# GpSimd's operations wait for the VectorE operation that the plan put before them at the shared port

## The chip, the cores and the metric

One core of a Trainium2 chip runs one program. The metric is the device time of one execution in microseconds (us): median of three runs 697.6, from 697.25 to 699.5. One further execution was profiled; it took 697.67.

The engines: TensorE (PE, its weight loads PEld) multiplies into PSUM, VectorE (DVE) and ScalarE (ACT) read PSUM and SBUF, GpSimd (POOL) works on SBUF alone, SyncE (SP) issues DMAs. Each engine runs its own queue in order and waits on semaphores that others raise.

## The reference

Attention with a threshold, then a gated mix, all in float32 (8 batches, 8 heads, 576 positions, 64 wide):

```python
scores = scale * np.matmul(q, k.transpose(0, 1, 3, 2))
thresh = np.max(scores, axis=-1, keepdims=True) - tau
scores = np.where(scores >= thresh, scores, -1000000000.0)
attn = np.exp(scores - np.max(scores, axis=-1, keepdims=True))
attn = attn / (np.sum(attn, axis=-1, keepdims=True) + 1e-09)
x = np.matmul(attn, v)   # heads side by side: (8, 576, 512)
gate_pre = sum(conv_w[k] * xp[:, k:k + S] for k in range(5))   # xp: x behind 4 rows of zeros
out = (1 / (1 + np.exp(-gate_pre))) * (x @ w_val) @ w_out
```

## The kernel before

The heads go in 32 pairs (8 batches of 4). Per pair nine score tiles, most of 128 x 576, are made by TensorE (L594), scaled into SBUF with their largest value by VectorE (L601, tile sb), and turned into weights: a threshold th (L611 on VectorE or GpSimd, L609 on ScalarE), an exponential e on ScalarE (L617, L619), and the cut, either on VectorE (L636: keeps e where sb is under th, tile pp or pl, with the row's sum) or on ScalarE (L630). L657 takes reciprocals of the sums, L667 on GpSimd or L665 on ScalarE widens them to inv, TensorE turns the weights (L724), ScalarE copies them out (L736), TensorE multiplies by v (L797), and VectorE writes the pair's xT (L806).

Then the pair's mix: xh and xl, the high and low part of xT (L840 or L342, and L846 on GpSimd), and the convolution: tap 0 on GpSimd (L859, tile pre), the others on VectorE (L864), in a few early pairs one of them as L879 and L885 on GpSimd. Per batch two products of 512 x 512 (L955), between them g (L993), its parts gh (L1016, ScalarE) and gl (L1024, GpSimd).

In the first 150 us the two weight matrices are also rebuilt from 64-bit words by `from_f64`: on VectorE L355, L357, L359, L361 and L368, on GpSimd L366, L371 and L417.

What sets the order: every piece is an `op` with an engine, a cost and a due number. `carry_out` plays all of them through once, at build time: it takes the operation that can begin first by the costs, moves the engine's clock on, and at the end emits all in that order. VectorE has two names there. "DVE" is an operation with an operand in PSUM (or a tiny one); "DVEp" is one on SBUF alone, with two large inputs or int32 words. DVEp and POOL share one clock, `port`: in the plan no two of them ever run at the same time. The emitted program knows nothing of `port`: an operation waits for its data and its rooms (the buffers, `Rooms`), and for nothing else.

Of the kernel before, what the change touches and what calls it, by code (L numbers as in the profile page):

```python
# [33 lines left out]
for x in range(6):  # L34
# [10 lines left out]
    s=3,  # L45
# [33 lines left out]
def tile_thresholded_attention_gated_mix(  # L79
# [14 lines left out]
    nc = tc.nc  # L94
# [86 lines left out]
    port = [0.0]  # L181
# [15 lines left out]
    def keep_busy(room, n, x=ident):  # L197

        for _ in range(n):
            nc.tensor.matmul(room[:, 0:P], x, x, start=True, stop=True)  # L200

    def sent(t, n, latency, each):

        at = t
        for _ in range(n):
            if len(landings) >= 8:
                at = max(at, landings[-8])
            wire[0] = max(wire[0], at + latency) + each
            landings.append(wire[0])
            at += SEND  # L210
        return at - t, wire[0] - t

    def carry_out():
        done_ops = []
        while True:
            best = None
            for e, ops in open_ops.items():
                can = []
                free = idle[e.rstrip("p")]
                if e in ("DVEp", "POOL"):  # L220
                    free = max(free, port[0])
                for o in ops:
                    if all(r.times for r in o.takes):
                        can.append((max([free, o.ready] + [r.times[0] for r in o.takes]), o))
                if can:
                    t = min(x for x, _ in can)
                    o = min((x[1] for x in can if x[0] <= t), key=lambda o: o.due)
                    if best is None or (t, o.due) < (best[0], best[1].due):
                        best = (t, o, e)
            if best is None:  # L230
                break
            t, o, e = best
            for x in o.ways:
                open_ops[x].remove(o)
            if e == "PE" and 0.0 < idle["PE"] and t < FILL_UNTIL and r_s.times:
                pause = t - max(idle["PE"], r_s.times[0])
                if pause > 0.8:
                    o.fill = int((pause - 0.6) / 0.24)
            cost, done, emit = o.ways[e]
            if e == "PE" and cost:  # L240
                extra = CHANGE.get((shape[0], o.shape), 0.0)
                cost, done = cost + extra, done + extra
                shape[0] = o.shape
            if isinstance(done, tuple):
                cost, done = sent(t, *done)
            if e in ("DVEp", "POOL"):
                port[0] = t + cost
            e = e.rstrip("p")
            idle[e] = t + cost
            o.landed, o.engine = t + done, e  # L250
            done_ops.append((o, emit))
            for r in o.takes:
                r.times.pop(0)
            for r, _ in o.gives:
                r.times.append(o.landed)
                r.times.sort()
            for n in o.next:
                n.ready = max(n.ready, idle["PE"] if e == "PE" and e in n.ways else o.landed)
                n.waits -= 1
                if not n.waits:  # L260
                    for x in n.ways:
                        open_ops[x].append(n)
        assert not any(open_ops.values()), "some operations can never begin"
        for o, emit in done_ops:
            if o.fill:
                keep_busy(r_s.free[0][1][:, 0, :], o.fill)
            emit()
            for rooms, room in o.gives:
                rooms.give(room(), o.landed)

# [244 lines left out]
    class Tile:  # L515
        s = None
# [45 lines left out]
        def room(self):  # L562

            if self.s is None:
                self.s = self.grp.second
            return self.s
# [536 lines left out]
    at = 0  # L1103
# [6 lines left out]
    for t in jobs:  # L1110
# [21 lines left out]
        if t.pair.g == NP - 1:  # L1132
            last = products(batch, len(tiles), last)
    carry_out()


# [57 lines left out]
```

## Time and profile before

| | |
|---|---|
| median of the runs | 697.6 us |
| profiled execution | 697.67 us |
| its span | 695.9 us |
| PE busy | 664.3 us |
| DVE busy | 596.1 us |
| ACT busy | 587.4 us |
| POOL busy | 249.5 us |

The span is what the profile covers; 1.8 us of the execution lie around it. "Busy" is time in which the engine has an instruction running, also one that is held up, which shows as one that took long. The chain of work that ended last goes back from the last instruction, at each step to what released it. A row of the timeline gives start, duration, engine, line, operation and tiles; a bracket at its end is idle time of that engine before it and what ended it. From about 170 us on the rows repeat with each batch, every 81.0 us.

### The profile page before, as it was taken

How to read it: one execution, taken by the hardware profiler on the slowest of the kernel's cores; microseconds unless marked ns; L12 is line 12 of the kernel's file. 1: busy time of each engine (PE TensorE's matmuls, PEld its weight loads, DVE VectorE, ACT ScalarE, POOL GpSimd, SP SyncE). 2: the span in 40 equal slices, each digit the busy share in tenths (PEclk: the TensorE clock that was granted, in tenths of full speed). 3: DMA queues.
4: the chain of work that ended last, by engine and by line, in shares of the span. 5: the costliest groups of instructions: out<-in, count | busy, mean ns of one | idle time of the engine just before them, and what ended most of it. 6: DMA issues, size and time to landing. Idle time of an engine off the chain costs nothing.

```text
span 695.9 us, 21477 instructions
## 1 busy us (share of the span) xinstructions
PE 664.3 (95%) x8610; PEld 521.8 (75%) x8610; DVE 596.1 (86%) x1598; ACT 587.4 (84%) x1206; POOL 249.5 (36%) x404
## 2 busy tenths in 40 slices
PE   8877889999999999999999999999999999999997
PEld 5544557667887777888787788877778887777897
DVE  6988989998888898988979989888989889799642
ACT  6998989999889988998879989799889988799620
POOL 2554555673222620433222422226214332224231
PEclk9999999999999999999999999999999999999999
DMA  7123333023321233223222233311332232220102
GB/s 266 51 96 108 123 116 103 33 70 117 118 87 29 78 120 102 84 86 103 64 94 86 68 120 103 103 40 66 120 106 82 85 104 75 83 86 1 53 19 70
DMA packets 21076, 61.19 MB, mean 88 GB/s; under 512 B 2928, under 2 KB 4336, under 8 KB 20976
## 3 DMA queue, kind: packets, MB, share of 16 engines
q1 hardware_dynamic: 20832, 59.62, 25.3%
q8 instruction: 68, 1.11, 0.7%
q14 instruction: 32, 0.26, 0.1%
q10 hardware_dynamic: 144, 0.20, 0.1%
HBM read 50.37 MB, written 9.44 MB: 86 GB/s over the span
## 4 chain that ended last, share of the span: by engine, by line
PE 53%; DVE 27%; ACT 13%; issue 6%; DMA 0%; DVEq 0%; ACTq 0%
PE u L955 19%; PE u L797 14%; DVE sb L601 12%; PE u L594 11%; DVE pp L636 8%; PE u L724 7%; ACT e L619 3%; ACT T L736 3%; ACT pp L630 3%; PE u L768 2%; ACT e L617 2%; DVE pre L864 2%; DVE r L657 1%; DVE pl L636 1%; ACT inv L665 1%
## 5 line engine op out<-in xcount | busy, mean ns | idle before, releaser
L601 DVE TENSOR_SCALAR_CACHE_REDUCE sb<-u,sc 128x576 f32<-128x576 f32 x288 | 228.0, 809 | 26.2 <-PE u L594 13.9
L594 PE MATMUL u<-k,q 64*128 64x288 f32 x1240 | 190.0, 418 | 5.1 <-DVE sb L601 3.3
L736 ACT COPY T<-u 128x512 f32<-128x512 f32 (+1 forms) x256 | 169.9, 688 | 13.2 <-PE u L724 12.4
L636 DVE SCALAR_TENSOR_TENSOR pp<-sb,th,e 128x577 f32<-128x577 f32 x164 | 145.0, 892 | 16.1 <-ACT e L619 15.3
L619 ACT ACTIVATE e<-sb,nm 128x576 f32<-128x576 f32 x193 | 146.6, 772 | 3.5 <-DVE sb L601 1.3
L797 PE MATMUL u<-T,v 128*64 128x256 f32 (+1 forms) x1080 | 136.9, 408 | 2.0 <-ACT T L736 2.0
L724 PEld LDWEIGHTS u<-ident,pp 64*128 64x128 f32 x2304 | 102.8, 139 | 46.1 <-ACT T L736 9.8
L594 PEld LDWEIGHTS u<-k,q 64*128 64x128 f32 x1240 | 108.4, 187 | 29.5 <-DVE sb L601 8.9
L724 PE MATMUL u<-ident,pp 64*128 64x64 f32 x2304 | 114.7, 226 | 15.3 <-DVE sb L601 7.8
L797 PEld LDWEIGHTS u<-T,v 128*64 128x64 f32 x1080 | 75.1, 137 | 54.4 <-ACT T L736 3.1
L864 DVE SCALAR_TENSOR_TENSOR pre<-xT,cw,pre 128x576 f32<-128x576 f32 x121 | 107.7, 890 | 1.7 <-POOL pre L859 0.9
L955 PE MATMUL u<-xh,wvh 64*128 64x288 f32 x512 | 87.3, 326 | 0.9 <-ACT seen L943 0.3
L955 PE MATMUL u<-gh,woh 64*128 64x288 f32 x512 | 84.1, 316 | 0.9 <-ACT T L744 0.6
L617 ACT ACTIVATE e<-sb,th 128x576 f32<-128x576 f32 x95 | 73.3, 775 | 8.0 <-DVE th L611 5.3
L955 PE MATMUL u<-xh,wvl 64*128 64x288 f32 x512 | 78.7, 291 | 0.0
L955 PE MATMUL u<-xl,wvh 64*128 64x288 f32 x512 | 78.6, 291 | 0.0
L955 PE MATMUL u<-gh,wol 64*128 64x288 f32 x512 | 77.9, 291 | 0.0
L955 PE MATMUL u<-gl,woh 64*128 64x288 f32 x512 | 77.9, 291 | 0.0
L630 ACT ACTIVATE pp<-e,minus 128x576 f32<-128x576 f32 x92 | 71.2, 774 | 0.7 <-DVE pp L636 0.2
L1024 POOL TENSOR_TENSOR gl<-g,gh 128x288 fp32r<-128x288 f32 x64 | 58.9, 935 | 31.8 <-ACT gh L1016 31.6
L667 POOL TENSOR_SCALAR inv<-r 128x128 f32<-128x128 f32 x79 | 25.0, 316 | 123.8 <-DVE r L657 106.1
L955 PEld LDWEIGHTS u<-xh,wvh 64*128 64x128 f32 x512 | 51.1, 185 | 6.4 <-DVE xT L806 3.3
(92 smaller groups left out, 992.7 us busy)
## 6 DMA issues: line engine op xcount, KB each, us to landing
q<-qT SPq DMA_DIRECT2D x31, 608.0 KB, 4.1
k<-kT SPq DMA_DIRECT2D x31, 496.0 KB, 5.0
v<-vs SPq DMA_DIRECT2D x32, 320.0 KB, 2.9
outT<-o SPq DMA_DIRECT2D x28, 288.0 KB, 2.2
pre<-w_val SPq DMA_DIRECT2D x4, 512.0 KB, 6.9
pre<-w_out SPq DMA_DIRECT2D x4, 512.0 KB, 3.5
outT<-o SPq DMA_DIRECT2D x8, 144.0 KB, 1.8
pp<-first SPq DMA_DIRECT2D x2, 192.0 KB, 3.0
```

The source lines that it names most:

```text
L594: nc.tensor.matmul(row(self.s)[:, a, :], t.q[rows, x : x + P], t.k[rows, k0 : k0 + HS], start=i == 0, stop=h is not None or i == 1, skip_g ...
L601: nc.vector.tensor_scalar(self.sb[:, :S].rearrange("p (a f) -> p a f", a=2), row(self.room()), sc, None, op0=ALU.mult, op1=ALU.min, accum_ ...
L617: nc.scalar.activation(y, x, AF.Prelu, bias=self.th, scale=-1.0, alpha=STEEP)
L619: nc.scalar.activation(y, x, AF.Exp, bias=self.nm, scale=-1.0)
L630: nc.scalar.activation(grp.p[:, i * S : (i + 1) * S], self.e[:, :S], AF.Exp, bias=minus, accum_out=grp.sums[:, i : i + 1])
L636: nc.vector.scalar_tensor_tensor(grp.p[:, i * S : (i + 1) * S + 1], self.sb, self.th, self.e, op0=ALU.is_le, op1=ALU.mult, accum_out=grp.s ...
L724: nc.tensor.transpose(tp[:, r, i * APART_BY : i * APART_BY + D], x[rows, :], ident[rows, rows])
L736: engine(T[:, c0 : c0 + n, self.off : self.off + P].rearrange("p c (r q) -> p r c q", r=2), tp)
L797: nc.tensor.matmul(a[hs, : W[half.j]], t.v[:, c0 : c0 + D], half.T[:, 2 * NKC if c == NKC else h * NKC + c, 0 : W[half.j]], start=c == 0, ...
L864: engine.scalar_tensor_tensor(cv, pair.xT[:, i + a : i + z], cw[:, g, i : i + 1], cv, op0=ALU.mult, op1=ALU.add)
L955: nc.tensor.matmul(made["room"][:, to, 0:HS], wt[rows, c, e * P : (e + 1) * P], moving(c, i)[rows, parts[j]], start=turn == c == n == 0, s ...
L1024: engine.tensor_sub(gs[e][1][:, c], g[x][:, c], gs[e][0][:, c].bitcast(F32))
```

## The change

`carry_out` notes on each operation whether it is a DVEp or a POOL one. While it emits them, it remembers the last DVEp instruction, and every GpSimd operation that comes after it gets a semaphore wait for that instruction to be done. VectorE gets no new wait, and none for GpSimd.

```diff
+            o.port = e if e in ("DVEp", "POOL") else None
+            if o.port:
                 port[0] = t + cost
...
+        shared = None
         for o, emit in done_ops:
...
+            n = len(nc.cur_bb.bb.instructions)
             emit()
+            made = [x for x in nc.cur_bb.bb.instructions[n:]] if o.port else ()
+            if made and o.port == "POOL" and shared:
+                tc.add_manual_dep(
+                    made[0], shared.name, mybir.DependencyInfo(mybir.DependencyClass.Sync, mybir.DependencyReason.DATA),
+                    reason="VectorE's turn at the shared port is over",
+                )
+            elif made and o.port == "DVEp":
+                shared = made[0]
```

The order on all five engines stays as it was. On GpSimd's queue, 68 of 409 rows get a wait for VectorE that had none, 15 lose theirs (one in front of them now covers it), and others wait for a later VectorE instruction than before. Lines below 243 keep their numbers, the others are 11 higher after the change.

The first place is GpSimd's queue at 21 us, where a weight block is put together (L366 and L371 before, L377 and L382 after). Before:

```order
L667 TENSOR_SCALAR inv1_130<-r0_126 128x128 [waits DVE_49,PE_49,Activation_49]
L366 TENSOR_TENSOR wvh_90<-wvh_90,o0_161 128x512 [waits Activation_49]
L371 TENSOR_TENSOR whole0_169<-whole0_169,wvh_90 128x512 [waits Pool_49]
L342 TENSOR_SCALAR pl0_120<-pl0_120 128x64 [waits DVE_49,PE_49]
L611 TENSOR_SCALAR th3_116<-nm3_112,less_87 128x1 [waits DVE_49]
```

After:

```order
L678 TENSOR_SCALAR inv1_130<-r0_126 128x128 [waits DVE_49,PE_49,Activation_49]
L377 TENSOR_TENSOR wvh_90<-wvh_90,o0_161 128x512 [waits DVE_49,Activation_49]
L382 TENSOR_TENSOR whole0_169<-whole0_169,wvh_90 128x512 [waits DVE_49,Pool_49]
L353 TENSOR_SCALAR pl0_120<-pl0_120 128x64 [waits PE_49]
L622 TENSOR_SCALAR th3_116<-nm3_112,less_87 128x1 [waits DVE_49]
```

The two sums now wait for VectorE (the first for the cut into pp, the second for the cut into pl behind it), and the copy in pl behind them no longer needs a wait of its own for that.

The second place is GpSimd's queue at 285 to 300 us, the low parts gl of one batch; the same rows come in each later batch. Before:

```order
L1024 TENSOR_TENSOR gl0_157<-g0_151,gh0_153 128x288 [waits Activation_49]
L1024 TENSOR_TENSOR gl0_157<-g0_151,gh0_153 128x288
L342 TENSOR_SCALAR pl0_120<-pl0_120 128x64 [waits DVE_49]
L667 TENSOR_SCALAR inv0_129<-r1_127 128x128 [waits DVE_49,PE_49,Activation_49]
L611 TENSOR_SCALAR th0_113<-nm0_109,less_87 128x1 [waits DVE_49]
L1024 TENSOR_TENSOR gl1_158<-g1_152,gh1_154 128x288 [waits Activation_49]
L611 TENSOR_SCALAR th1_114<-nm1_110,less_87 128x1 [waits DVE_49]
L1024 TENSOR_TENSOR gl1_158<-g1_152,gh1_154 128x288
L667 TENSOR_SCALAR inv0_129<-r0_126 128x128 [waits DVE_49,PE_49,Pool_49]
```

After:

```order
L1035 TENSOR_TENSOR gl0_157<-g0_151,gh0_153 128x288 [waits DVE_49,Activation_49]
L1035 TENSOR_TENSOR gl0_157<-g0_151,gh0_153 128x288 [waits DVE_49]
L353 TENSOR_SCALAR pl0_120<-pl0_120 128x64 [waits DVE_49]
L678 TENSOR_SCALAR inv0_129<-r1_127 128x128 [waits DVE_49,PE_49,Activation_49]
L622 TENSOR_SCALAR th0_113<-nm0_109,less_87 128x1 [waits DVE_49]
L1035 TENSOR_TENSOR gl1_158<-g1_152,gh1_154 128x288 [waits Activation_49]
L622 TENSOR_SCALAR th1_114<-nm1_110,less_87 128x1 [waits DVE_49]
L1035 TENSOR_TENSOR gl1_158<-g1_152,gh1_154 128x288 [waits DVE_49]
L678 TENSOR_SCALAR inv0_129<-r0_126 128x128 [waits DVE_49,PE_49,Pool_49]
```

Three of the four gl rows get a wait for VectorE: the two halves of gl0 for a cut (L636) each, the second half of gl1 for a tap (L864), the second one of three that stand in VectorE's queue there.

## Rows read from the trace of the kernel before

**Rows 1.** The page: shares of the chain that ended last, by engine.
```profile
PE 53%; DVE 27%; ACT 13%; issue 6%; DMA 0%; DVEq 0%; ACTq 0%
```

**Rows 2.** Busy time in stretches: stretch, length, then busy us by engine.
```profile
22.00:40.00 18.00, 13.44 (x160) 8.91 (x156) 17.93 (x49) 16.34 (x33) 9.71 (x12) 1.00 0.41 140
...
280.60:299.60 19.00, 18.50 (x246) 14.27 (x242) 18.20 (x48) 18.20 (x40) 5.47 (x12) 1.00 0.20 65
299.60:342.00 42.40, 42.40 (x570) 34.52 (x572) 37.98 (x101) 37.34 (x78) 16.17 (x27) 1.00 0.26 91
```

**Rows 3.** Lines L636 and L864: shortest/median/longest ns; L656 among the groups.
```profile
L636 DVE SCALAR_TENSOR_TENSOR pp<-sb,th,e x164: 800/819/1843, 8.2 to 652.0; 128x577 f32<-128x577 f32 x164
L864 DVE SCALAR_TENSOR_TENSOR pre<-xT,cw,pre x121: 796/814/1935, 35.6 to 668.4; 128x576 f32<-128x576 f32 x121
L656 DVE TENSOR_SCALAR sums<-sums 128x1 f32<-128x1 f32 (+1 forms) x77 | 12.7, 164 | 2.1 <-ACT pp L630 1.3
```

**Rows 4.** Timeline, 8 to 40 us, of VectorE, GpSimd and ScalarE.
```profile
21.92 1.84 DVE L636 SCALAR_TENSOR_TENSOR pp<-sb,th,e 128x577 f32<-128x577 f32 x1
35.60 1.94 DVE L864 SCALAR_TENSOR_TENSOR pre<-xT,cw,pre 128x576 f32<-128x576 f32 x1
...
21.78 1.36 POOL L366 TENSOR_TENSOR wvh<-wvh,o 128x512 fp32r<-128x512 f32 x1 [1.09 <-ACT wvh L364]
...
25.19 0.78 ACT L617 ACTIVATE e<-sb,th 128x576 f32<-128x576 f32 x1 [0.82 <-DVE th L611]
39.36 0.30 ACT L665 COPY inv<-r 128x128 f32<-128x128 f32 x1 [0.77 <-DVE r L657]
```

**Rows 5.** Timeline, 46 to 62 us, VectorE and ScalarE.
```profile
53.00 1.65 DVE L636 SCALAR_TENSOR_TENSOR pp<-sb,th,e 128x577 f32<-128x577 f32 x1
...
57.34 0.78 ACT L617 ACTIVATE e<-sb,th 128x576 f32<-128x576 f32 x1 [0.46 <-DVE pp L636]
```

**Rows 6.** Timeline, 98 to 108 us, of VectorE, GpSimd and ScalarE.
```profile
100.08 0.81 DVE L864 SCALAR_TENSOR_TENSOR pre<-xT,cw,pre 128x576 f32<-128x576 f32 x1
100.81 1.24 DVE L656 TENSOR_SCALAR sums<-sums 128x2 f32<-128x2 f32 x1
...
100.25 1.77 POOL L371 TENSOR_TENSOR whole<-whole,woh 128x512 f32<-128x512 f32 x1 [1.62 <-DVE woh L368]
...
102.28 0.30 ACT L665 COPY inv<-r 128x128 f32<-128x128 f32 x1 [1.52 <-DVE r L657]
```

**Rows 7.** Timeline, 127 to 139 us, VectorE and ScalarE.
```profile
135.78 1.35 DVE L636 SCALAR_TENSOR_TENSOR pp<-sb,th,e 128x577 f32<-128x577 f32 x1
...
137.31 0.30 ACT L665 COPY inv<-r 128x128 f32<-128x128 f32 x1 [1.00 <-DVE r L657]
```

**Rows 8.** Timeline, 282 to 300 us: VectorE, GpSimd, ScalarE in one batch.
```profile
293.19 1.38 DVE L864 SCALAR_TENSOR_TENSOR pre<-xT,cw,pre 128x576 f32<-128x576 f32 x1
...
295.23 0.81 DVE L864 SCALAR_TENSOR_TENSOR pre<-xT,cw,pre 128x576 f32<-128x576 f32 x1
...
296.22 1.65 DVE L864 SCALAR_TENSOR_TENSOR pre<-xT,cw,pre 128x576 f32<-128x576 f32 x2
298.19 0.49 DVE L806 TENSOR_TENSOR xT<-u,T 128x320 f32<-128x320 f32 x1 [0.32 <-PE u L797]
...
293.15 0.80 POOL L1024 TENSOR_TENSOR gl<-g,gh 128x288 fp32r<-128x288 f32 x1
299.36 0.30 POOL L667 TENSOR_SCALAR inv<-r 128x128 f32<-128x128 f32 x1 [5.41 <-DVE r L657]
...
295.40 0.78 ACT L617 ACTIVATE e<-sb,th 128x576 f32<-128x576 f32 x1 [0.21 <-DVE pp L636]
296.34 0.30 ACT L665 COPY inv<-r 128x128 f32<-128x128 f32 x1 [0.16 <-DVE r L657]
```

**Rows 9.** Timeline, 305 to 322 us, GpSimd: the last gl of the batch, what follows.
```profile
314.20 2.16 POOL L1024 TENSOR_TENSOR gl<-g,gh 128x288 fp32r<-128x288 f32 x2 [0.67 <-ACT gh L1016]
319.87 0.30 POOL L667 TENSOR_SCALAR inv<-r 128x128 f32<-128x128 f32 x1 [3.52 <-DVE r L657]
```

More of the change, by code (lines that the diff above doesn't have):

```diff
@@ L245, in carry_out @@
                 cost, done = sent(t, *done)
-            if e in ("DVEp", "POOL"):
+            o.port = e if e in ("DVEp", "POOL") else None
+            if o.port:
                 port[0] = t + cost
```

## The prediction, made before the changed kernel ran

> **What bounds the kernel now.** I read the chain first, then busy time by stretch, then the slow single operations. The chain is TensorE for 53%, VectorE for 27%, ScalarE for 13% [rows 1]: no engine bounds throughout. The stretches say where which does [rows 2]. From 299.6 to 342 us TensorE is busy 42.40 of 42.40 us; time won on another engine there is worth nothing. From 280.6 to 299.6 us it is busy 18.50 of 19.00, VectorE 18.20 and ScalarE 18.20: three engines hand work round with next to no slack. Stretches like these two come in every batch from 200 us on. From 22 to 40 us VectorE is busy 17.93 of 18.00, ScalarE 16.34, TensorE 13.44: here VectorE sets the pace.
>
> The single operations show what the change is about. L636 takes 819 ns in the median and 1843 at worst, L864 814 and 1935, the same shape each time [rows 3]. The long ones stand beside a GpSimd operation that began earlier: L636 at 21.92 us took 1.84 us, and L366 on GpSimd had run from 21.78 for 1.36 [rows 4]; L864 at 293.19 took 1.38, and L1024 on GpSimd had run from 293.15 for 0.80 [rows 8]. In both, VectorE ended 0.62 us after GpSimd (23.76 against 23.14, and 294.57 against 293.95), which is less than the 0.82 that its operation needs; with GpSimd's spans drawn some 0.2 long, VectorE stood until GpSimd let go. The plan had GpSimd's operation behind VectorE's; on the chip it came a hair earlier and won.
>
> **The change part by part.** It adds no work and moves nothing. It makes GpSimd wait, in these cases, for the VectorE operation it blocked, so that VectorE's surplus over 0.82 us goes. What that is worth depends on who is late next, so I set each surplus against the idle time of ScalarE behind it, which is the other full engine.
>
> First, 22 to 40 us [rows 4]. Surplus on VectorE 1.84 - 0.82 = 1.02, and 1.94 - 0.82 = 1.12 for L864 at 35.60, in all 2.14. ScalarE idles 0.82 (until 25.19, for a th from VectorE) and 0.77 (until 39.36, for r) behind them, 1.59 in all; the rest of the surplus meets a busy ScalarE. Term: 1.59.
>
> Second, 53 us [rows 5]. Surplus 1.65 - 0.82 = 0.83; ScalarE idles 0.46 behind it, for L636. Term: 0.46.
>
> Third, 100 us [rows 6]. L656, which adds 1e-9 to two sums, took 1.24 us where the mean is 0.164 [rows 3]: L371 on GpSimd was issued at 100.25, in the middle of an L864, and took the port when that ended. L656 is not among the operations that the plan counts at the port. But L371 will now wait for the L864 in front, from 100.08 to 100.89. That end is what releases it, while L656 shows as begun at 100.81, before that end: it is already at VectorE's door when L371 is let go. So L656 should slip through first. Surplus 1.08, ScalarE idle 1.52 behind it. Term: 1.08, and nothing if L371 wins after all.
>
> The Trainium skill (SBUF — State Buffer, section "SBUF: two separate sides") says that VectorE and GpSimd hold one port pair as an exclusive lock for a whole instruction, that whoever starts first gets it, and that VectorE wants it with two SBUF inputs or in a 2-port perf mode. The trace agrees on the lock (L636 at 1.84) and on a one-input operation standing there (L656 at 1.24). It speaks against the change in one point: a lock that GpSimd takes right behind VectorE's operation blocks the next VectorE operation, counted in the plan or not. By that rule, with L371 first at the lock, the third term would be 0 instead of 1.08 and the time 694.6, which is still the forecast's case.
>
> Fourth, 136 us [rows 7]. Surplus 1.35 - 0.82 = 0.53, ScalarE idle 1.00 behind it, for r. Term: 0.53.
>
> Fifth, the repeated stretch of 280.6 to 299.6 us, five times alike, 81.0 us apart [rows 2, 8]. Surplus of L864 at 293.19: 1.38 - 0.82 = 0.56. Behind it ScalarE idles 0.21 (until 295.40) and 0.16 (until 296.34) and is busy otherwise, so 0.37 gets through to the matmuls of 299.6. Term: 5 x 0.37 = 1.85.
>
> Sum of the gains: 1.59 + 0.46 + 1.08 + 0.53 + 1.85 = 5.51.
>
> Now what the added waits cost. The queue behind a waiting GpSimd operation waits too. The second half of gl1, from 293.15, must now wait for the second L864, which ended at 296.04 and will end some 0.56 earlier: 2.3 us late. Behind it stands inv at 299.36, before which GpSimd idled 5.41 us [rows 8]: hidden, cost 0. The last gl of the batch (314.20 to 316.36) waits for a later tap as well, by some 2.5 us; behind it GpSimd idled 3.52 [rows 9], and TensorE, which reads gl, is in its full stretch: cost 0. If that cover were gone, each us of lateness would go straight to TensorE.
>
> What is not free: GpSimd's operation, let go by one VectorE operation, holds the port against the next one. In the repeated stretch the gl1 half would start at 295.5 or a little later and hold the third L864 (296.22, then 295.66) for about 0.7; VectorE has 0.32 of idle time before L806 at 298.19 and L806 itself can begin no more than 0.37 earlier, so at most 0.1 is lost, inside my rounding. In the early part, where GpSimd's work is dense (9.71 of 18 us), I can't place every new meeting. I take one full operation, as long as L366, 1.36 [rows 4], for all of them; the ends are 0 (each falls beside VectorE's PSUM work) and four of them, 5.4.
>
> Forecast: 697.67 - 5.51 + 1.36 = 693.5 us. The profiled execution is 0.07 above the median of the runs, so this compares with 697.6 as it stands.
>
> **The rivals.** *Handed on nowhere.* ScalarE and TensorE are nearly full where VectorE is; TensorE idles only 0.50 of the 19.00 us [rows 2]. If ScalarE's small gaps close by other waits, the repeated term goes, and of the early ones only half stay: 697.67 - (3.66 / 2) = 695.8. For it: all three engines full. Against: ScalarE's gaps have VectorE as their releaser by name. The case in which the change does nothing that matters, because GpSimd stood at the port anyway and the new wait takes the place of the old one, ends in the same range.
>
> *All surplus comes off.* If ScalarE's work also moves up because it was itself late through VectorE, the whole surplus counts: 2.14 + 0.83 + 1.08 + 0.53 + 5 x 0.56 = 7.38, or 690.3. Against: ScalarE has no idle time before most of it.
>
> *The stall moves and grows (slower).* A GpSimd operation that starts right behind VectorE's holds the next VectorE operation for its full length, where before it held one for the remainder. Place: the third L864 of the repeated stretch, 0.2 us behind the one that lets GpSimd go. Price there: 0.80, less the 0.32 idle before L806, 0.48 lost, five times, 2.4; and in the early part each of the three surpluses at L636 and L864 (1.02, 1.12, 0.83) is replaced by a full 1.36, 1.1 lost in sum. 697.67 + 2.4 + 1.1 = 701.2. It decides from the point where the gap between the VectorE operation waited for and the next one at the port is under 0.8 us in most places. For it: the taps lie that close. Against: between cuts stands PSUM work (L601), which the plan counts at no port.
>
> **How the numbers follow.** Forecast 0.57, all surplus 0.13, handed on nowhere 0.19, slower 0.11. The likeliest gives 693.5. A measurement of this kernel tells about 0.3% from no change, 2.1 us, so faster is under 695.5: 0.57 + 0.13 = 0.70; same 0.19; slower 0.11. The range runs from 689.0 (all surplus, and as much again as one place that I haven't listed) to 697.5 (handed on nowhere, with the moved stall of 1.36 and a little more): it leaves out the slower rival and a bit of the fast one.
>
> **What would show it.** In the changed profile L636 and L864 at worst near 1.4 us, not 1.9, their busy sums lower; L636 at 21 us, L864 at 34 and at 292 us at 0.82; L656 at 100 us at 0.16. ScalarE's waits for VectorE at 25, 39, 57, 102 and 137 us gone or shorter. GpSimd idle for VectorE's L636 and L864 where it was idle for nothing, without TensorE, ScalarE or VectorE waiting for GpSimd. The stretch of 299.6 us should begin some 4 us earlier and be 42.4 us long as before. I am wrong if L864 at 296.22 grows by 0.8 and L806 behind it comes later, or if th or inv from GpSimd turn up among the longest waits.

## The result, and the profile after

The changed kernel takes 689.35 us in the median (688.32 to 691.7, six runs) where the kernel before takes 697.88 beside it (697.07 to 699.5, six runs): 8.5 us less, a ratio of 0.9877 with a 95% interval of 0.9857 to 0.9897. The forecast was 693.5, so the sign was right and the forecast gain half of what came; the range of 689.0 to 697.5 just holds it. The profiled execution took 689.33.

The page of the changed kernel, busy time and the chain that ended last (lines after the change are 11 higher: L647 is the old L636, L875 the old L864, L1035 the old L1024):

```profile
PE 660.4 (96%) x8610; PEld 521.0 (76%) x8610; DVE 586.8 (85%) x1598; ACT 586.7 (85%) x1206; POOL 229.6 (33%) x404
...
PE 67%; DVE 15%; ACT 13%; issue 4%; POOL 0%; DMA 0%; DVEq 0%; ACTq 0%; POOLq 0%
```

VectorE's share of the chain fell from 27% [rows 1] to 15%, and TensorE's rose from 53% to 67%. VectorE is busy 9.3 us less, GpSimd 19.9 us less. Neither does less work; both stood less, since time for which an instruction is held up at the port counts as busy.

Busy time in stretches of the changed kernel (stretch, length, then PE, PEld, DVE, ACT, POOL), and the lines of the cut and the tap with their shortest, median and longest ns:

```profile
22.00:40.00 18.00, 15.42 (x184) 10.22 (x182) 17.81 (x55) 17.96 (x37) 9.35 (x13) 1.00 0.42 142
...
274.50:293.50 19.00, 18.61 (x248) 14.52 (x246) 17.97 (x48) 18.63 (x41) 5.84 (x13) 1.00 0.20 64
293.50:335.90 42.40, 42.40 (x582) 34.88 (x580) 37.95 (x101) 37.38 (x77) 14.54 (x26) 1.00 0.27 91
```

```profile
L647 DVE SCALAR_TENSOR_TENSOR pp<-sb,th,e x164: 807/818/1357, 8.1 to 643.7; 128x577 f32<-128x577 f32 x164
...
L875 DVE SCALAR_TENSOR_TENSOR pre<-xT,cw,pre x121: 797/814/1766, 34.7 to 660.0; 128x576 f32<-128x576 f32 x121
```

From 22 to 40 us ScalarE went from 16.34 [rows 2] to 17.96 of 18.00 and TensorE from 13.44 to 15.42. TensorE's full stretch is as long as before, 42.40 of 42.40, and begins at 293.5 in place of 299.6. The longest cut fell from 1843 to 1357 ns [rows 3]; the longest tap, 1766 for 1935, shows that stalls are still there.

Where the time went I read from VectorE, whose queue has the same order in both kernels: the start of the same operation before and after.

| VectorE operation | before | after | earlier by |
|---|---|---|---|
| tap | 38.20 | 36.22 | 1.98 |
| xT | 45.20 | 41.62 | 3.58 |
| xT | 65.83 | 61.71 | 4.12 |
| xT | 96.28 | 92.03 | 4.25 |
| r | 102.08 | 96.76 | 5.32 |
| o | 137.86 | 132.05 | 5.81 |
| sb | 200.34 | 194.74 | 5.60 |
| cut, one batch on | 286.80 | 280.70 | 6.10 |
| cut, five batches on | 611.00 | 603.13 | 7.87 |
| last tap | 668.36 | 660.03 | 8.33 |

5.6 us are won by 200 us and 0.45 in each of the six repeated stretches that follow.

**The first stretch.** Timeline of the changed kernel, 19 to 46 us, VectorE, then GpSimd; the last line is VectorE's in the kernel before:

```profile
21.87 0.81 DVE L647 SCALAR_TENSOR_TENSOR pp<-sb,th,e 128x577 f32<-128x577 f32 x1
...
34.72 0.83 DVE L875 SCALAR_TENSOR_TENSOR pre<-xT,cw,pre 128x576 f32<-128x576 f32 x1
...
39.90 1.77 DVE L875 SCALAR_TENSOR_TENSOR pre<-xT,cw,pre 128x576 f32<-128x576 f32 x1
41.62 0.49 DVE L785 TENSOR_TENSOR xT<-u,T 128x320 f32<-128x320 f32 x1
...
22.84 1.27 POOL L377 TENSOR_TENSOR wvh<-wvh,o 128x512 fp32r<-128x512 f32 x1 [2.20 <-DVE pp L647]
...
39.77 1.28 POOL L382 TENSOR_TENSOR whole<-whole,wvh 128x512 f32<-128x512 f32 x1
...
41.88 1.35 DVE L864 SCALAR_TENSOR_TENSOR pre<-xT,cw,pre 128x576 f32<-128x576 f32 x1
```

The cut of 1.84 us takes 0.81 and the tap of 1.94 takes 0.83 [rows 4]. L377 now begins when the cut has ended, and its bracket names that cut as releaser. The tap at 39.90 is stalled for longer than before: it took 1.35 at 41.88 and takes 1.77 now, and L382 began 0.13 us before it.

Then, between the tap at 38.20 and the xT at 45.20 of the table, 1.6 us appear that no stall explains. TensorE in the kernel before, and its granted clock (PEclk, third from the end of a stretch's row):

```profile
40.05 0.69 PE L724 MATMUL u<-ident,pp 64*128 64x64 f32 x10 [1.62 <-DVE sb L601]
...
40.77 4.31 PE L768 MATMUL u<-T,v 128*64 128x320 f32 x20
```

```profile
41.00:42.00 1.00, 1.00 (x6) 0.41 (x6) 0.96 (x4) 1.00 (x2) 1.00 (x2) 0.50 0.00 0
42.00:43.00 1.00, 1.00 (x8) 0.41 (x6) 1.00 (x1) 1.00 (x3) 0.62 (x1) 0.50 0.06 16
```

The same two views of the changed kernel:

```profile
38.07 0.52 PE L735 MATMUL u<-ident,pp 64*128 64x64 f32 x10 [0.73 <-DVE sb L612]
...
38.59 2.91 PE L779 MATMUL u<-T,v 128*64 128x320 f32 x20
```

```profile
39.00:40.00 1.00, 1.00 (x12) 0.50 (x10) 0.96 (x5) 1.00 (x2) 1.00 (x2) 1.00 0.11 25
40.00:41.00 1.00, 1.00 (x10) 0.56 (x8) 1.00 (x1) 1.00 (x3) 1.00 (x1) 1.00 0.00 0
```

Before, TensorE had idled 1.62 us for a late sb and then ran at a granted clock of 0.50, 1.2 GHz; the twenty matmuls by v took 4.31 us. After, it idled 0.73, stayed at 1.00, 2.4 GHz, and the same twenty took 2.91. That is 1.40 us, beside a pause that got 0.89 shorter. The kernel before has two more such spells, near 61 and 92 us; the changed one has them too, near 58 and 88.

**One batch.** Timeline of the changed kernel, 284 to 294 us, VectorE, GpSimd, ScalarE:

```profile
287.00 0.81 DVE L875 SCALAR_TENSOR_TENSOR pre<-xT,cw,pre 128x576 f32<-128x576 f32 x1
...
289.47 2.17 DVE L875 SCALAR_TENSOR_TENSOR pre<-xT,cw,pre 128x576 f32<-128x576 f32 x2
292.00 0.49 DVE L817 TENSOR_TENSOR xT<-u,T 128x320 f32<-128x320 f32 x1 [0.37 <-PE u L808]
...
289.37 0.80 POOL L1035 TENSOR_TENSOR gl<-g,gh 128x288 fp32r<-128x288 f32 x1 [2.36 <-DVE sums L667]
292.96 0.30 POOL L678 TENSOR_SCALAR inv<-r 128x128 f32<-128x128 f32 x1 [2.79 <-DVE r L668]
...
289.03 0.78 ACT L628 ACTIVATE e<-sb,th 128x576 f32<-128x576 f32 x1
```

The first tap, 1.38 us before [rows 8], takes 0.81. The second half of gl1, held until the second tap was done (its bracket names the small sum that ended beside it), begins at 289.37, and the two operations from 289.47 on take 2.17 where they took 1.65: 0.57 won and 0.52 given back. ScalarE's idle time of 0.21 [rows 8] before this e is gone.

### The profile page after: what moved, and what is told of

Its sections match the earlier page's. It is cut to its first block, busy times and chain, and to the rows that moved or that the text cites. A ratio compares the mean times of both kernels' runs of the same rounds, so it can differ in the third digit from the quotient of the medians.

```text
span 687.5 us, 21500 instructions
## 1 busy us (share of the span) xinstructions
PE 660.4 (96%) x8610; PEld 521.0 (76%) x8610; DVE 586.8 (85%) x1598; ACT 586.7 (85%) x1206; POOL 229.6 (33%) x404
## 4 chain that ended last, share of the span: by engine, by line
PE 67%; DVE 15%; ACT 13%; issue 4%; POOL 0%; DMA 0%; DVEq 0%; ACTq 0%; POOLq 0%
PE u L966 22%; PE u L808 19%; PE u L605 14%; PE u L735 9%; DVE sb L612 7%; DVE pp L647 4%; ACT e L630 3%; ACT T L747 2%; ACT pp L641 2%; ACT e L628 2%; PE u L779 1%; DVE pl L647 1%; DVE r L668 1%; DVE pre L875 1%; ACT th L620 1%
## 5 line engine op out<-in xcount | busy, mean ns | idle before, releaser
L647 DVE SCALAR_TENSOR_TENSOR pp<-sb,th,e 128x577 f32<-128x577 f32 x164 | 140.1, 862 | 16.6 <-ACT e L630 15.9
L875 DVE SCALAR_TENSOR_TENSOR pre<-xT,cw,pre 128x576 f32<-128x576 f32 x121 | 104.2, 861 | 3.0 <-POOL pre L896 1.3
L1035 POOL TENSOR_TENSOR gl<-g,gh 128x288 fp32r<-128x288 f32 x64 | 54.6, 855 | 69.5 <-ACT gh L1027 25.0
L966 PEld LDWEIGHTS u<-gh,woh 64*128 64x128 f32 x512 | 51.2, 185 | 6.4 <-DVE xT L817 1.7
```

Of the source, the lines that this page charges most:

```text
L647: nc.vector.scalar_tensor_tensor(grp.p[:, i * S : (i + 1) * S + 1], self.sb, self.th, self.e, op0=ALU.is_le, op1=ALU.mult, accum_out=grp.s ...
L875: engine.scalar_tensor_tensor(cv, pair.xT[:, i + a : i + z], cw[:, g, i : i + 1], cv, op0=ALU.mult, op1=ALU.add)
L966: nc.tensor.matmul(made["room"][:, to, 0:HS], wt[rows, c, e * P : (e + 1) * P], moving(c, i)[rows, parts[j]], start=turn == c == n == 0, s ...
L1035: engine.tensor_sub(gs[e][1][:, c], g[x][:, c], gs[e][0][:, c].bitcast(F32))
```

## Experiments

All are variants of the changed kernel. Most keep some of its waits: GpSimd's operations are numbered in the order in which they are emitted, and a condition on that number picks those that wait. Each variant's line numbers are shifted by its own edit: against the kernel before by 13 where waits are picked, by 18 where VectorE waits as well, by 30 where operations are emitted later.

### The first 47 us, 47 to 175, and the rest

```diff
+        nth = -1
...
+            nth += o.port == "POOL"
...
-            if made and o.port == "POOL" and shared:
+            if made and o.port == "POOL" and shared and nth < 30:
```

The second has `30 <= nth < 113` there, the third `nth >= 113`.

> The added waits on the first 30 GpSimd operations behind the set-up alone (up to about 47 us), none after. Theory: the stalls at 21.9 and 35.6 us go, the matmuls at 40 us start 2.0 us earlier, and TensorE keeps its full clock through the 20 matmuls behind them, another 1.6 us: 3.6 us in all, kept to the end, so about 694.2, with one spell of half clock fewer than before. Rival (the clock is an accident, and only the waits count): about 2.0 us, 695.8. Rival (the early gain is swallowed by the full engines behind it): under 1 us, 697.

> The added waits on GpSimd's operations from about 47 to 175 us alone. Theory: the stalls at 53, 79, 101 and 136 us go and give what the changed kernel gained between 46 and 200 us, 2.1 us: about 695.7, spells of half clock as before. Rival (the gains there need the first stretch to have moved): no more than 1 us, 696.8.

> The added waits from 175 us on alone. Theory: each repeated stretch gives 0.45 us, six of them, 2.7 us: about 695.1. Rival (the stalls come off but the freed GpSimd operation blocks the next tap instead): 0, 697.8.

| waits kept | median us | ratio to the kernel before | us won |
|---|---|---|---|
| up to 47 us | 694.42 | 0.9946 (0.9929 to 0.9962) | 3.56 |
| 47 to 175 us | 695.40 | 0.9958 (0.9942 to 0.9974) | 2.58 |
| later | 695.01 | 0.9953 (0.9935 to 0.9972) | 2.97 |

The median of before was 697.98. Each of the three came within 0.5 us of its theory, and their intervals leave out the rivals' gains of 2.0, 1 and 0. The three add up to 9.1, the whole gives 8.5; the product of the ratios, 0.9858, lies at the edge of the whole's interval. So the gain is spread over the run, and the stretches hardly lean on each other.

### Two waits alone

The condition is `nth in (10, 20)`: the two weight sums that stood beside the cut at 21.92 and the tap at 35.60.

> Of the changed kernel's waits only the two of the weight sums (L366 before the change) at 21.8 and 35.5 us are kept; GpSimd's other operations wait as in the kernel before. Theory: these two make all of the gain of the first 47 us: L636 at 21.92 and L864 at 35.60 at 0.82 us (1.03 and 0.94 won), and with that TensorE's spell at half its clock at 40.2 us is gone, which is worth some 1.6 us more: 3.6 less than the kernel before, 694.3 us. Rival 1: the other waits up to 47 us shape the work in front of TensorE's pause, and the two alone leave the spell where it is: 2.0 less, 695.9. Rival 2: the spell only moves to a later place: 2.0 less too, with a spell that the kernel before does not have.

693.61 us (693.11 to 693.84, five runs) against 697.95, ratio 0.9933 (0.9921 to 0.9945): 4.3 us from two waits. (Between the two profiles 0.30 us stand ahead of the first of them.) TensorE's timeline of that kernel, and its clock:

```profile
37.61 0.53 PE L737 MATMUL u<-ident,pp 64*128 64x64 f32 x10 [0.50 <-DVE sb L614]
...
38.12 2.91 PE L781 MATMUL u<-T,v 128*64 128x320 f32 x20
```

```profile
40.00:41.00 1.00, 1.00 (x10) 0.32 (x6) 1.00 (x1) 1.00 (x3) 1.00 (x2) 1.00 0.05 16
```

The pause is 0.50 us and the spell is gone, without any of the other waits, and no spell stands where the kernel before has none. Both rivals fall. What came above the expected 3.6 is the cut at 53.00 us: it goes from 1.65 to 0.81 though the GpSimd operation beside it waits as in the kernel before. Moved by 4 us, it missed it.

### The same two, and all waits after 47 us

The condition is `(nth in (10, 20) or nth >= 30)`.

> As the changed kernel, but of the thirty GpSimd operations of the first 47 us only the two weight sums wait (at 21.8 and 35.5 us); all later waits are kept. The two alone gave 4.3 us, all thirty 3.6, the waits behind them 2.6 and 3.0. Theory: the other early waits only push stalls about, and what the two alone won by more comes on top: 0.5 to 1.3 less than the changed kernel, 688.0 to 688.9 us. Rival: what the two alone won by more was L636 at 53 us, which the later waits take off anyway, so nothing comes on top: as the changed kernel, 689.4.

688.49 us (688.28 to 688.62, four runs), ratio 0.9859 (0.9836 to 0.9881). The median fits the theory, but the interval overlaps the changed kernel's (0.9857 to 0.9897). Of 0.95 us between the two profiles 0.53 stand before 7 us, ahead of every wait that differs; 0.40 come from two operations at 34.72 and 42.02 us. Whether dropping the other 28 early waits gains anything stays open.

### One wait alone: L371 at 100 us

The condition is `nth == 60`.

> A single wait is kept, that of GpSimd's L371 at 100 us for the L864 in front of it. Theory: L656 at 100.81 goes from 1.24 to 0.16 us and slips through before L371, and some 0.9 of it stays by 140 us: 0.9 less than the kernel before, 697.0 us. Rival 1: L371 then stands in front of a later VectorE operation for its full length and the whole is given back within 10 us: same time, 697.9. Rival 2: TensorE loses a pause by it and with it a spell at half its clock: 2.4 less, 695.5.

698.93 us (697.87 to 700.45, twelve runs) against 697.95, ratio 1.0012 (1.0002 to 1.0022): nothing won, and by the interval 0.1 to 1.5 us lost. Timeline of this kernel, 101 to 110 us, VectorE, then GpSimd:

```profile
102.26 0.16 DVE L669 TENSOR_SCALAR sums<-sums 128x2 f32<-128x2 f32 x1
...
106.44 1.28 DVE L649 SCALAR_TENSOR_TENSOR pl<-sb,th,e 128x577 f32<-128x577 f32 x1
107.65 1.24 DVE L669 TENSOR_SCALAR sums<-sums 128x2 f32<-128x2 f32 x1
...
102.43 1.28 POOL L384 TENSOR_TENSOR whole<-whole,woh 128x512 f32<-128x512 f32 x1 [2.34 <-DVE sums L669]
...
107.47 1.39 POOL L430 TENSOR_TENSOR wol<-whole,woh 128x512 fp32r<-128x512 f32 x1 [0.37 <-ACT woh L427]
```

The two-column sum at 102.26 does slip through first, 0.16 for 1.24 us [rows 6]. But GpSimd's four large operations behind it came later too, and two of them met other work: a cut takes 1.28, and the next two-column sum the same 1.24, beside a GpSimd operation that began 0.18 earlier. Rival 1, then: the stall moved. In the changed kernel these operations wait as well, and the gain stays. Its timeline, 94 to 105 us:

```profile
96.57 0.16 DVE L667 TENSOR_SCALAR sums<-sums 128x2 f32<-128x2 f32 x1
...
101.49 0.16 DVE L667 TENSOR_SCALAR sums<-sums 128x2 f32<-128x2 f32 x1
...
96.74 1.28 POOL L382 TENSOR_TENSOR whole<-whole,woh 128x512 f32<-128x512 f32 x1 [2.11 <-DVE sums L667]
...
101.64 0.73 POOL L857 TENSOR_TENSOR xl<-xT,xh 128x256 fp32r<-128x256 f32 x1 [1.43 <-DVE sums L667]
```

### The repeated stretch: second half of gl1 alone, gl0 alone

The conditions are `nth >= 113 and nth % 46 == 133 % 46` (six waits) and `nth >= 113 and nth % 46 in (34, 35)`.

> One added wait per batch from 200 us on: the second half of gl1 (L1024) waits for the tap (L864) in front, six waits in the program. Theory: nearly all of the repeated gain hangs on this one, ScalarE's idle times behind that tap being what it closes: 2.2 to 2.7 us, about 695.4. Rival (the other eight waits of each batch carry it, above all the ones that free L636 and L864 at 307 to 316 us): under 0.5 us, 697.4.

> Only the waits of the two halves of gl0 are kept, in the six stretches from 200 us on. Theory: what gl1 did not give comes from here: L636 at 286.80 goes from 0.99 to 0.82 us, and the 0.17 stay, six times: 1.0 less than the kernel before, 696.9 us. Rival 1: all that is left of the 0.45 a batch, 0.25 each, hangs on gl0 alone: 1.5 less, 696.4. Rival 2: the 0.17 are given back at the next full engine: same time, 697.9.

gl1: 696.9 us (twelve runs), ratio 0.9987 (0.9973 to 1.0). gl0: 697.63 (twelve runs), ratio 0.9991 (0.9979 to 1.0002). By the times alone neither is clear of no change. By the traces gl1 gives 0.2 a batch: 0.57 at the first tap, 0.52 given back at the third, and 0.2 made up again in the 6 us behind it. gl0 takes the cut at 286.80 from 0.99 to 0.81, 0.17, of which the next sb gives back 0.09 in most batches. My theory that gl1 carries nearly all fell, and so did that of 0.17 a batch for gl0: the traces leave about 0.09 of it. The rest of the 0.45 shows in the traces of before and after at the tap behind the last gl (314.47, 1.23 us before, 0.81 after), 0.42 less 0.25 given back; that wait was not tried alone.

### The gl1 half still later

The second half of gl1 is emitted behind the last tap of that place, and so waits for that one. (Four taps stand there and not three: the row at 296.22 [rows 8] holds two.)

```diff
+            o.begun, o.took = t, cost
...
+            if not (nth >= 113 and nth % 46 == 133 % 46):
+                continue
...
+                if y.port == "DVEp" and y.begun < o.begun + o.took + 2.0:
+                    to = x
...
+            done_ops.insert(to, done_ops.pop(i))
```

> The changed kernel, with the second half of gl1 in the six batches from 200 us on waiting for the last of the three taps (L864) there, not for the second: it then meets no tap at all. Theory (what the wait gives at the second tap, 0.57 us, is given back at the third, 0.52, and only part of it reaches TensorE): the third tap falls from 1.32 to 0.82 us and each of six stretches gives 0.2 us more, 1.2 in all, about 688.1. Rival (ScalarE is full behind the third tap, and L806 waits for TensorE anyway): the tap falls, the time stays at 689.4. Rival (GpSimd comes too late for inv behind it): slower, 690 or more.

689.25 us (four runs), ratio 0.9868 (0.9849 to 0.9887): as the changed kernel. VectorE's timeline:

```profile
289.43 1.65 DVE L894 SCALAR_TENSOR_TENSOR pre<-xT,cw,pre 128x576 f32<-128x576 f32 x2
291.97 0.49 DVE L836 TENSOR_TENSOR xT<-u,T 128x320 f32<-128x320 f32 x1 [0.89 <-PE u L827]
```

The moved stall is gone, 2.17 to 1.65 us. And xT behind it begins at 291.97 where it began at 292.00 in the changed kernel: VectorE's idle time for TensorE grew from 0.37 to 0.89. In the repeated stretch that stall cost nothing; the full TensorE sets the time of xT. The rival held.

### VectorE waits for GpSimd as well

Each operation at the port now also waits for the last GpSimd operation in front of it in the plan, so both engines take the turns of the plan.

```diff
             elif made and o.port == "DVEp":
                 shared = made[0]
+                if passed:
+                    tc.add_manual_dep(made[0], passed.name, ...)
+            if made and o.port == "POOL":
+                passed = made[0]
```

> The changed kernel, and each VectorE operation that the plan counts at the port also waits for the GpSimd operation in front of it in the plan: the order of the plan is held both ways. Theory (the gain is that VectorE, the fuller engine, no longer stands; GpSimd is late but has idle time): VectorE now stands for a late GpSimd, above all before 200 us, and half or more of the gain goes: 693 to 696. Rival (the plan's order is worth holding as such): as the changed kernel or faster, 689.4 or under.

698.3 us (twelve runs), ratio 1.0 (0.9988 to 1.0012): the whole gain is gone. Its cut, L654 here, and the three largest of VectorE's waits for GpSimd (us in total, times, longest):

```profile
L654 DVE SCALAR_TENSOR_TENSOR pp<-sb,th,e x164: 810/818/824, 7.8 to 653.0; 128x577 f32<-128x577 f32 x164
```

```profile
DVE pre L882 <- POOL gl L1042: 9.4, 13, 0.9
DVE pp L654 <- POOL xl L864: 6.6, 7, 1.0
DVE pp L654 <- POOL xh L360: 4.8, 6, 0.8
```

Not one of 164 cuts is stalled, the longest takes 824 ns, and the kernel is no faster than with stalls of up to 1843. The lost time moved from "busy" to "waits": 20.8 us in these three groups. Keeping the two engines from meeting is therefore not by itself what gained; the gain came with waits on GpSimd's side alone. Part of what is lost here is TensorE's clock: this trace has a spell at 0.50 from 39.5 us on, as the kernel before has, where the changed kernel has none.

### Every large GpSimd operation later

Each GpSimd operation of over 0.5 us is emitted behind the VectorE operations that the plan starts up to 0.3 us after its end, and waits for them.

```diff
+            if not (o.took > 0.5):
+                continue
...
+                if y.port == "DVEp" and y.begun < o.begun + o.took + 0.3:
+                    to = x
```

> The changed kernel, with each GpSimd operation of over 0.5 us waiting not for the VectorE operation in front but for the next one at the port behind it too, where the plan lets that one begin within 0.3 us of GpSimd's end. Theory (stalls left in the changed kernel are ones where GpSimd starts right in front of the next VectorE operation): they go as well, some 4 us of stalls before 200 us of which half counts, and 0.2 us in each later stretch: about 686.5. Rival (GpSimd's lateness now reaches TensorE through its thresholds, inverses and low parts): slower than the changed kernel, 691 or more.

706.76 us (706.35 to 707.1, four runs), ratio 1.0127 (1.0106 to 1.0147): 17 above the changed kernel. The theory (686.5) fell; the rival had the sign. The largest waits for GpSimd in it:

```profile
ACT e L647 <- POOL th L641: 5.5, 6, 0.9
DVE pre L894 <- POOL pre L915: 3.6, 2, 2.1
DVE pre L894 <- POOL pre L889: 2.9, 3, 1.1
```

The same waits in the changed kernel, all of them but two of 0.3 us:

```profile
DVE g L1004 <- POOL gl L1035: 2.7, 4, 1.0
DVE pre L875 <- POOL pre L896: 1.3, 1, 1.3
DVE pre L875 <- POOL pre L870: 0.9, 1, 0.9
```

ScalarE waits six times, up to 0.9 us, for a small th of GpSimd, and VectorE 3.6 and 2.9 for the convolution's part on GpSimd, where the changed kernel has 1.3 and 0.9. TensorE waits once, 1.4 us, for GpSimd's pl, which it never does in the changed kernel. How the 17 us divide between such waits and new stalls was not taken apart.

## Why the prediction was half right

**The mechanism held.** VectorE stood for GpSimd, and the waits let it go first: L636 at 21.92 us and L864 at 293.19 at 0.81, L656 at 100.81 at 0.16, as the prediction said. ScalarE's and TensorE's waits for GpSimd hardly grew (0.3 in the changed kernel, on ScalarE), and VectorE's grew by 1.3. gl1 was 2.4 us late (its bracket says 2.36), against 2.3, and GpSimd still idled 2.79 before inv.

**First term, 1.59: too small.** It capped a surplus of 2.14 by the idle time of ScalarE straight behind the two stalls. 1.98 came through. VectorE was busy 17.93 of 18.00 us there [rows 2], so it was the one that set the pace, and ScalarE closed gaps elsewhere in the stretch too, to 17.96. The cap was read from the wrong engine.

**Not in the sum: TensorE's clock.** By the traces about 1.4 us of the gain are a spell at 1.2 GHz that is gone. The two waits alone bear it out: 4.3 us, of which 2.15 are the two stalls and 0.84 the cut at 53.00, and a mean granted clock of 0.995 in all five runs, which the kernel before reached in 3 of the 65 runs that stand beside the experiments. That the shorter pause is the reason was not shown; the last section has traces that speak against its length alone. I read the stretch from 22 to 40 us and stopped at the edge; the clock of the microseconds behind it stood in the profile of the kernel before.

**Second, third and fourth terms: sizes near, one reason missing.** From 45 to 66 us 0.54 came (0.46 said), from 96 to 102 us 1.07 (1.08), from 102 to 138 us 0.49 (0.53). The second fits in part by luck: the cut at 53.00 gave its full 0.84 and the tap at 57.23, which no term names, 0.60, while a sum of two columns and a cut that stand longer now (at 42.02 and 52.19) took back 0.46 and 0.40. The third is right in size, and its reason, that L656 slips through before L371, holds. But that wait alone gave nothing: the stall moved 6 us on. The term needed the waits behind it, which the prediction had as a cost only.

**Fifth term, 5 x 0.37: too small, and for a wrong reason.** It is 6 x 0.45. By the traces the six waits of gl1's second half, on which it rested, gave some 0.2 each; the rest is some 0.09 from gl0, which I had not costed, and some 0.17 behind the last gl, and neither of these shows in times of its own. Counting five stretches and not six, with 200 us the first, left out another 0.45.

**The moved stalls, +1.36: they came, and in the repeated stretch did not count.** At least six did, among them the tap at 39.90 (1.77 us) and the third tap of each batch, grown by 0.52 where I had 0.7. A longer third tap with a later xT behind it was to show me wrong. It grew, and xT (L817) came 6.19 us earlier all the same; as 6.10 of these stood already before the stretch (the cut at 286.80), xT's place alone would not settle it, but the later gl1 showed that the full 0.52 is covered by TensorE. In the early part two of them did take time back (0.46 and 0.40, above), but inside the sizes measured there; to deduct a whole operation on top was as large an error as the clock.

**The rivals.** The slower one (701.2) takes place at the third tap as described and costs nothing there. "All surplus comes off" (690.3) came nearest to the time, by luck: the measured time has 1.4 of clock, and moved stalls, that its sum does not name. The low end of the range held by luck too: it left room for one place not listed, and the clock filled that room.

The Trainium skill (SBUF — State Buffer, section "SBUF: two separate sides") says that whoever starts first has the port pair for the whole instruction. The runs agree: L382 began 0.13 us before the tap at 39.90, which took 1.77. By it the third term might have been 0; the sum of two columns got there first (0.16).

## What to carry to other kernels

Where two engines meet at one port, let the one off the path wait for the one on it, and not the other way: one-sided waits gave 8.5 us here, waits on both sides nothing, and still later GpSimd work cost 9 against the kernel before. Look at what the delayed operation meets next: a single wait only moved the meeting (L656, nothing won), while two waits at the right places gave half of the whole gain (4.3 us). And before capping a gain by the gaps behind it, look which engine is full in that stretch, and at TensorE's granted clock right after its next pause.

## What the runs showed of the hardware that I had not expected

A TensorE pause of 1.62 us was followed by matmuls at a granted clock of 0.50, one of 0.73 or 0.50 us in the same place was not; the difference was 1.40 us on twenty matmuls. The length of the pause alone does not decide it. TensorE in the kernel whose waits begin only behind 175 us, at the same place, with its clock:

```profile
39.90 0.46 PE L737 MATMUL u<-ident,pp 64*128 64x64 f32 x8 [1.64 <-ACT T L749]
41.48 0.52 PE L737 MATMUL u<-ident,pp 64*128 64x64 f32 x10 [1.12 <-DVE sb L614]
41.99 2.91 PE L781 MATMUL u<-T,v 128*64 128x320 f32 x20
...
42.00:43.00 1.00, 1.00 (x10) 0.62 (x10) 1.00 (x5) 1.00 (x3) 1.00 (x1) 1.00 0.00 0
```

Pauses of 1.64 and 1.12 us, and the clock stays at 1.00; in the kernel where VectorE waits as well, one of 1.22 there is followed by 0.50. What else decides stays open. Such spells go with part of the spread between runs. With the mean granted clock of a run at 0.990 the kernel before took 699.3 us in the mean (21 runs), at 0.995 696.5 (three runs). At 0.995 the changed kernel took 688.3 and 689.0, so some 7.8 of the 8.5 us are there at one clock too. That leaves 0.7 for the clock where the two traces gave 1.4; five runs are too few to say which.

A tiny operation can stand at the port for as long as GpSimd holds it. The sum on 128 x 2, 0.16 us as a rule, took 1.24 beside L371 (100.81 [rows 6]) and beside L430 (107.65, above), and 0.62 at 42.02 in the changed kernel. The sum on 128 x 1 took its usual time everywhere, also inside GpSimd's operations: in the kernel before 13 of 59 ran inside one of over 0.6 us, such as the one at 46.81, 0.15 us, inside an xl that ran from 46.60 to 47.33. The two forms in the kernel with every large GpSimd operation later (busy us, mean ns):

```profile
L686 DVE TENSOR_SCALAR sums<-sums 128x1 f32<-128x1 f32 x59 | 8.6, 146 | 2.6 <-ACT pp L660 2.5
L686 DVE TENSOR_SCALAR sums<-sums 128x2 f32<-128x2 f32 x18 | 6.3, 352 | 1.8 <-ACT pp L660 1.8
```

146 ns is also the mean of the one-column form in the kernel before, where the two-column form has 223.
